# Tail stores from two hardware queues at once, and tail pairs one place earlier

## The chip, the cores and the metric

The kernel runs on one core of a Trainium2 chip. The metric is device time in microseconds (us), the median of several runs. Before the change it is 433.02 us (three runs, 432.55 to 433.25). The profile's span counts from the first to the last instruction and is about 2 us shorter than the device time. Times inside a trace are us from that span's start.

## The reference

Linear attention (8 batches, 8 heads, 576 positions, head size 64) gives `x`. A spectral mixing step with 64 complex modes and 128 weight matrices of 512x512, read from HBM as f32, gives `y`. Then comes a small channel product:

```python
X = np.fft.rfft(x, axis=1)
Yr = einsum(Xr, w_r) - einsum(Xi, w_i);  Yi = einsum(Xr, w_i) + einsum(Xi, w_r)   # 64 modes
u = x + np.fft.irfft(Y, n=576, axis=1)
out = u + np.maximum(u @ w_ch, 0.0)        # [8, 576, 512] f32, 9.4 MB
```

## The kernel before

Each batch has 576 rows. 512 of them make four full tiles (`x_main`, 128 partitions). The 64 left over are the tail: the tails of two batches share one tile (`x_tail`), one batch on partitions 0 to 63, the other on 64 to 127. In the last stage tiles go in pairs: TensorE adds the inverse transform and the channel product in PSUM (`channels`, `rectified`, `finish`), ScalarE applies the relu, VectorE adds to `x`, and a store follows. 16 pairs are main pairs, 2 are tail pairs.

```python
    pairs = []
    for b in range(B):
        pairs += [(b * NJJ, b * NJJ + 1), (b * NJJ + 2, b * NJJ + 3)]
        if b % 4 == 3:
            k = b // 4
            pairs.insert(len(pairs) - 1, (B * NJJ + 2 * k, B * NJJ + 2 * k + 1))
    # ...
    def store(t: int, n_t: int):
        if t < B * NJJ:                       # main: 128 partitions, 4 KB runs for a pair
            b, jj = divmod(t, NJJ)
            nc.sync.dma_start(
                out=out[b, 0:512, :].rearrange("(r j) d -> r j d", j=NJJ)[:, jj : jj + n_t, :],
                in_=x_main[b][:, jj : jj + n_t, :],
            )
            return
        i = t - B * NJJ                       # tail: two stores of 64 partitions, 2 KB runs
        for hf in range(2):
            (nc.sync, nc.gpsimd)[hf].dma_start(
                out=out[2 * i + hf : 2 * i + 4 : 2, 512:S, :].rearrange("b r d -> r b d"),
                in_=x_tail[i // 2][hf * 64 : hf * 64 + 64, :, :],
            )

    def finish(n: int):
        # ... inverse transform; the first and the last pair are stored tile by tile ...
        on_bank(n, {0, 1}, nc.vector.tensor_tensor(out=x, in0=acc, in1=x, op=ALU.add))
        store(t0, 2)
    # ...
    for n in range(4, len(pairs)):
        channels(n)
        rectified(n)
        finish(n - 1)
    finish(len(pairs) - 1)
```

Four of the experiments (e5, e7, e9, e10) touch the warm-up matmuls. These do no useful work; they are there to keep TensorE's granted clock up while the last weights arrive (from 388 to 394 us it is 1.00 with all of them and 0.74 in e5, which leaves part of them out):

```python
            if t == 1 and kk >= NM - 4:
                keep_warm(6)
        if NM - 4 <= kk < NM - 1:
            keep_warm(3)          # twice
```

Of the kernel before, what the change touches and what calls it, by code (L numbers as in the profile page):

```python
# [47 lines left out]
def kernel(  # L48
# [10 lines left out]
    nc = tc.nc  # L59

    B, H, S, Dh = q.shape
# [4 lines left out]
    NJJ = 4  # L66
# [61 lines left out]
    pin = tc.keep_in_program_order  # L128
# [279 lines left out]
    for kk in range(n_early):  # L408
# [5 lines left out]
    x_tail = [  # L414
        sW.tile([128, 2, D], F32, tag="x_tail", bufs=B // 4, name=f"x_tail{i}") for i in range(B // 4)
    ]
# [3 lines left out]
    def x_of(t: int):  # L420
        if t < B * NJJ:
            return x_main[t // NJJ][:, t % NJJ, :]
        i = t - B * NJJ
        return x_tail[i // 2][:, i % 2, :]
# [81 lines left out]
    def add_inverse(n: int, i: int, t: int, half: int, what: int = BOTH):  # L506

        acc = accs[n][:, i]
        mm = lambda o, l, r: on_bank(
            n, {i}, nc.tensor.matmul(o, l, r, start=False, stop=True, skip_group_check=True)  # L510
        )
        if t < B * NJJ:
            parts = [(t // NJJ, slice(0, 128), slice(t % NJJ * 128, t % NJJ * 128 + 128))]
        else:
            p = t - B * NJJ
            parts = [(2 * p + h, slice(h * 64, h * 64 + 64), slice(512, 576)) for h in range(2)]
        for b, r, sel in parts:
            if what == BOTH:
                mm(acc[r, :], inv_sb[:, sel], YZ[b][:, half, :])
                continue  # L520
            if what & EARLY:
                mm(acc[r, :], inv_sb[: 2 * NE, sel], YZ[b][: 2 * NE, half, :])
            if what & LATE:
                mm(acc[r, :], inv0_sb[:, sel], last[:, half, :])

    pairs = []
    for b in range(B):
        pairs += [(b * NJJ, b * NJJ + 1), (b * NJJ + 2, b * NJJ + 3)]
        if b % 4 == 3:
            k = b // 4  # L530
            pairs.insert(len(pairs) - 1, (B * NJJ + 2 * k, B * NJJ + 2 * k + 1))
    N_PRE = 2
    acc_pools: list = []
    users: dict[int, list] = {}
# [1 line left out]
    def on_bank(n: int, banks: set, ins):  # L536
        pin(ins)
        for other, theirs in users.setdefault(n, []):
            if not banks & theirs:
                tc.declare_no_dep(ins.ins, other.ins, reason="the other bank of the pair")  # L540
        users[n].append((ins, banks))
    accs: dict[int, object] = {}

    def channels(n: int):
        pool = acc_pools[n % 4 // 2]
        accs[n] = pool.tile([128, 2, D], F32, tag="acc", bufs=2, name=f"acc{n}")
        for i, t in enumerate(pairs[n]):
            for cols, src in e0_parts(t):
                on_bank(
                    n, {i},  # L550
                    nc.tensor.matmul(  # L551
                        accs[n][:, i, cols], id16, src, start=(cols.start == 0), stop=False,
                        skip_group_check=True,
                    ),
                )

    def rectified(n: int):
        for i, t in enumerate(pairs[n]):
            add_inverse(n, i, t, 1, LATE if n < N_PRE else BOTH)
        for i in range(2):  # L560
            a = accs[n][:, i]
            on_bank(n, {i}, nc.scalar.activation(out=a, in_=a, func=AF.Relu))  # L562

    def store(t: int, n_t: int):
        if t < B * NJJ:
# [5 lines that stand above are left out]
            return  # L571
        i = t - B * NJJ
        for hf in range(2):
            (nc.sync, nc.gpsimd)[hf].dma_start(
                out=out[2 * i + hf : 2 * i + 4 : 2, 512:S, :].rearrange("b r d -> r b d"),
                in_=x_tail[i // 2][hf * 64 : hf * 64 + 64, :, :],
            )

    def finish(n: int):
        acc = accs[n]  # L580
        single = n in (0, len(pairs) - 1)
        t0 = pairs[n][0]
        for i, t in enumerate(pairs[n]):
            if n < N_PRE:
                add_inverse(n, i, t, 0, EARLY)
                add_inverse(n, i, t, 0, LATE)
            else:
                add_inverse(n, i, t, 0)
            if single:
                x = x_of(t)  # L590
                on_bank(n, {i}, nc.vector.tensor_tensor(out=x, in0=acc[:, i], in1=x, op=ALU.add))  # L591
                store(t, 1)
        if single:
            return
        x = x_main[t0 // NJJ][:, t0 % NJJ : t0 % NJJ + 2, :] if t0 < B * NJJ else x_tail[(t0 - B * NJJ) // 2]
        on_bank(n, {0, 1}, nc.vector.tensor_tensor(out=x, in0=acc, in1=x, op=ALU.add))  # L596
        store(t0, 2)

    done = 0
    rows_done = 0  # L600
# [52 lines left out]
    rectified(1)  # L653
    channels(2)
    finish(0)
    channels(3)
    finish(1)
    rectified(2)
    rectified(3)
    finish(2)  # L660
    for n in range(4, len(pairs)):
        channels(n)
        rectified(n)
        finish(n - 1)
    finish(len(pairs) - 1)
    acc_pools[1].release()
# [30 lines left out]
```

## Time and profile before

| What | Value | Where it is read |
|---|---|---|
| weights until about 391 us | DMA share 1.08, 211 GB/s | stretches |
| start of the last weight matmuls | 394.05 us | timeline |
| full-rate stores, 405.3 to 409.3 us | 402 GB/s | stretches |
| VectorE's last add ends | 424.21 us | timeline |
| last store lands | 429.65 us | issue and landing events |

From the start of the last weight matmuls to the last landing it is 35.60 us. I use this length, the "store stage", because the start itself varies from run to run by more than the change can bring (393.86 to 394.99 us in these profiles).

These lines are from the view of stretches of the kernel before. The columns are the stretch, its length, each engine's busy time with its number of instructions, TensorE's granted clock, the DMA share and GB/s.

```profile
405.30:409.30 4.00, 4.00 (x25) 1.57 (x22) 3.56 (x3) 3.10 (x6) 0.00 (x0) 1.00 1.00 402
411.90:415.00 3.10, 3.10 (x16) 1.45 (x15) 2.89 (x4) 2.65 (x6) 0.00 (x0) 1.00 0.88 218
```

With main stores the DMA engines move 402 GB/s. Around the first tail pair they move 218 GB/s although they are 88% busy: the packets are slow, the engines are not idle. The next lines are the timeline of SyncE and GpSimd there (start, duration, engine, line, what is stored).

```profile
410.93 0.68 SPq L574 DMA_DIRECT2D out_dram<-x_tail  x1
412.26 0.33 SPq L567 DMA_DIRECT2D out_dram<-x_main  x1
411.20 0.63 POOL L574 DMA_DIRECT2D out_dram<-x_tail  x1 [10.47 <-DVE x_tail L596]
```

The next are DMA issues of single short windows of the kernel before. The last number is us from issue to landing. In order: the main store before the tail pair, the two halves, the main store after them, and the one issued at 416.14 us.

```profile
out_dram<-x_main SPq DMA_DIRECT2D x1, 512.0 KB, 2.6
out_dram<-x_tail SPq DMA_DIRECT2D x1, 256.0 KB, 3.2
out_dram<-x_tail POOLq DMA_DIRECT2D x1, 256.0 KB, 4.8
out_dram<-x_main SPq DMA_DIRECT2D x1, 512.0 KB, 5.0
out_dram<-x_main SPq DMA_DIRECT2D x1, 512.0 KB, 5.9
```

The time to landing is a gauge of backlog. It goes from 2.6 to 5.0 us across the tail pair and never returns, because TensorE makes a pair every 1.30 us and the DMA engines need about as long to store one.

The two halves do not run together. In the packet records of the trace, SyncE's half has its packets from 412.26 us (mean 158 ns for 2 KB) and GpSimd's from 413.55 us, 2.35 us after its issue.

### The profile page before, as it was taken

Reading aid. Unit: us, or ns where it says so; the run is one execution under the profiler, and the core shown is the slowest. Engines: PE = TensorE matmul, PEld = TensorE weight load, DVE = VectorE, ACT = ScalarE, POOL = GpSimd, SP = SyncE. Lnnn points to the kernel's source line nnn. Section 1 sums busy time; section 2 is a strip of 40 time slices with the busy share of each in tenths; the row PEclk is TensorE's granted clock in tenths of the full one; section 3 lists DMA queues with packets and bytes.
Section 4 is the critical chain, followed back from the end, with each engine's and each line's share of the span. In section 5 each row is a group of like instructions: output and inputs, shape, how many; then the busy total and the mean of one; then the engine's idle time right before and its main releaser. Section 6 shows DMA issues by size and latency. Waiting matters only on the chain. (4 is left out here: it accounts for less than half of the span.)

```text
span 430.9 us, 6215 instructions
## 1 busy us (share of the span) xinstructions
PE 297.7 (69%) x2542; PEld 154.3 (36%) x2542; DVE 176.9 (41%) x334; ACT 147.3 (34%) x228; POOL 92.3 (21%) x166
## 2 busy tenths in 40 slices
PE   0357867787018777677776767667787678997992
PEld 0346656564004233222322223222233226833440
DVE  0699998854004242322322222322223212202793
ACT  3587666631003222222223213222222221302781
POOL 4233232112102222211222112222212221200100
PEclk9996676666559766657658577566555866999997
DMA  8999999999999999999999999999999999993797
GB/s 148 207 208 209 209 209 209 211 213 215 222 211 213 216 212 213 213 213 213 213 214 214 213 213 213 214 214 214 214 214 213 213 213 213 214 213 77 292 330 281
DMA packets 35563, 92.38 MB, mean 214 GB/s; under 512 B 3152, under 2 KB 16336, under 8 KB 35536
## 3 DMA queue, kind: packets, MB, share of 16 engines
q0 software_dynamic: 32016, 82.52, 98.4%
q1 hardware_dynamic: 3520, 9.47, 5.9%
q8 instruction: 20, 0.33, 0.3%
q14 instruction: 7, 0.06, 0.0%
HBM read 164.07 MB, written 9.44 MB: 403 GB/s over the span
## 5 line engine op out<-in xcount | busy, mean ns | idle before, releaser
L468 PE MATMUL eps<-wch,xTw 128*128 128x512 f16 x144 | 61.4, 575 | 3.7 <-DVE xTw L465 3.2
L476 ACT CAST E<-eps 128x512 f16<-128x512 f32 (+1 forms) x40 | 21.3, 544 | 118.8 <-PE eps L468 118.8
L348 PE MATMUL P<-wr,xt_c 128*32 128x512 bf16 (+1 forms) x260 | 45.6, 560 | 23.5 <-DMA wr<-in_moe_w_r_dram 21.5
L348 PE MATMUL P<-wi,xt_c 128*32 128x512 bf16 (+1 forms) x260 | 44.7, 538 | 23.0 <-DMA wi<-in_moe_w_i_dram 23.0
L114 POOL DMA_DIRECT2D wi<-in_moe_w_i_dram x64 | 34.1, 532 | 122.1 <-PE P L348 86.3
L114 POOL DMA_DIRECT2D wr<-in_moe_w_r_dram x64 | 34.1, 532 | 119.0 <-PE P L348 96.8
L453 DVE TENSOR_TENSOR x_main<-nw,rd 128x256 f32<-128x256 f32 x64 | 24.1, 419 | 72.4 <-PE nw L146 72.4
L362 DVE CAST ys<-P 128x512 f16<-128x512 f32 (+1 forms) x33 | 22.5, 681 | 61.6 <-PE P L348 61.5
L348 PEld LDWEIGHTS <-xt_c 128*32 128x32 bf16 x520 | 24.8, 164 | 58.8 <-issue 28.3
L364 ACT CAST ys<-P 128x512 f16<-128x512 f32 (+1 forms) x32 | 18.5, 580 | 72.2 <-PE P L348 72.0
L146 PEld LDWEIGHTS <-qT 64*128 64x128 f16 (+1 forms) x640 | 20.6, 124 | 54.2 <-issue 38.7
L366 PE MATMUL yt<-pick_sb,ys 128*128 128x16 f16 x256 | 17.2, 176 | 32.1 <-DMA pick_sb<-row_pick 21.0
L465 DVE COPY xTw<-xTp 128x512 f16<-128x512 f16 x36 | 15.2, 423 | 46.0 <-PE xTp L463 46.0
L366 PEld LDWEIGHTS <-ys 128*128 128x128 f16 x256 | 13.2, 105 | 53.0 <-issue 24.8
L146 PE MATMUL num<-kv,qT 64*128 64x65 f16 (+1 forms) x320 | 12.9, 217 | 22.0 <-ACT kv L242 17.9
L468 PEld LDWEIGHTS <-xTw 128*128 128x128 f16 x144 | 14.6, 123 | 37.7 <-issue 23.6
L182 ACT ACTIVATE qe<-q 128x1152 f16<-128x1152 f16 x16 | 17.7, 1155 | 22.9 <-DMA q<-in_q_dram 22.9
L211 PE MATMUL qTp<-id,qe 128*128 128x128 f16 x144 | 16.7, 312 | 12.7 <-DVE qe L195 12.3
L460 ACT CAST x16w<-x_main 128x512 f16<-128x512 f32 x32 | 19.8, 619 | 13.0 <-DVE x_main L453 12.4
L265 DVE TENSOR_TENSOR x<-num,rd 128x512 f16<-128x512 f32 x32 | 22.1, 691 | 1.1
L463 PE MATMUL xTp<-id,x16w 128*128 128x128 f16 x144 | 19.5, 278 | 4.0 <-ACT x16w L460 4.0
L562 ACT ACTIVATE acc<-acc 128x512 f32<-128x512 f32 x36 | 19.1, 581 | 5.4 <-PE acc L510 3.8
(65 smaller groups left out, 382.8 us busy)
## 6 DMA issues: line engine op xcount, KB each, us to landing
wr<-in_moe_w_r_dram POOLq DMA_DIRECT2D x64, 512.0 KB, 18.2
wi<-in_moe_w_i_dram POOLq DMA_DIRECT2D x64, 512.0 KB, 18.4
out_dram<-x_main SPq DMA_DIRECT2D x14, 512.0 KB, 4.9
q<-in_q_dram POOLq DMA_DIRECT2D x8, 576.0 KB, 13.3
k<-in_k_dram POOLq DMA_DIRECT2D x8, 576.0 KB, 14.1
v<-in_v_dram POOLq DMA_DIRECT2D x8, 576.0 KB, 16.2
out_dram<-x_main SPq DMA_DIRECT2D x4, 256.0 KB, 4.0
wch<-in_moe_w_ch_dram POOLq DMA_DIRECT2D x1, 512.0 KB, 20.4
```

The source lines that it names most:

```text
L114: nc.gpsimd.dma_start(out=w, in_=src[kk].rearrange("(p dc) e -> p dc e", dc=NDC))
L146: mm = nc.tensor.matmul(num[hpo][orow, c0 : c0 + 65], qT[rows, hpp, h2, cols], kv_sb[rows, hpp, h2, :])
L265: nc.vector.tensor_tensor(out=dst.rearrange("p (o c d) -> p o c d", o=2, c=4), in0=nv[:, :, :, 0:64], in1=rden.unsqueeze(3).broadcast_to([ ...
L348: mm = nc.tensor.matmul(P[i][dc * 32 : dc * 32 + 32, :], xt_cols(dc, t, kk), w[:, dc, i * pw : i * pw + pw], start=(t == 1), stop=(t == 0) ...
L362: nc.vector.tensor_copy(out=dst, in_=P[i])
L366: mm = nc.tensor.matmul(yt_ps[:, ec, kk % 8, :], st[:, ec * 128 : ec * 128 + 128], pick_sb)
L453: nc.vector.tensor_tensor(out=x[orow, o * 256 : o * 256 + 256].rearrange("p (c d) -> p c d", c=4), in0=nv[o][:, :, 0:64], in1=rd_all[b][or ...
L460: nc.scalar.copy(out=x16, in_=x)
L463: nc.tensor.transpose(xT_ps[:, c, :], x16[:, c * 128 : c * 128 + 128], id16)
L468: nc.tensor.matmul(e_ps, xT[:, c, :], wch16[:, c, :], start=(c == 0), stop=(c == NDC - 1))
L476: nc.scalar.copy(out=dst, in_=e_ps[:, cols])
L562: on_bank(n, {i}, nc.scalar.activation(out=a, in_=a, func=AF.Relu))
```

## The change

The intent is to send the two halves of a tail pair together, on SyncE's and ScalarE's queues, which the profile lists as "hardware_dynamic" (GpSimd's is "software_dynamic"). ScalarE's store must not hold up its relus, so both wait until two pairs later. Hence the tail pairs move one place forward, or the second store would not fit in the loop.

```diff
-            pairs.insert(len(pairs) - 1, (B * NJJ + 2 * k, B * NJJ + 2 * k + 1))
+            pairs.insert(len(pairs) - 2, (B * NJJ + 2 * k, B * NJJ + 2 * k + 1))
...
-            (nc.sync, nc.gpsimd)[hf].dma_start(
-                out=out[2 * i + hf : 2 * i + 4 : 2, 512:S, :].rearrange("b r d -> r b d"),
-                in_=x_tail[i // 2][hf * 64 : hf * 64 + 64, :, :],
+            pin(
+                (nc.sync, nc.scalar)[hf].dma_start(
+                    out=out[2 * i + hf : 2 * i + 4 : 2, 512:S, :].rearrange("b r d -> r b d"),
+                    in_=x_tail[i // 2][hf * 64 : hf * 64 + 64, :, :],
+                )
             )
...
-        store(t0, 2)
+        if t0 < B * NJJ:
+            store(t0, 2)
...
         rectified(n)
+        if pairs[n - 2][0] >= B * NJJ:
+            store(pairs[n - 2][0], 2)
         finish(n - 1)
```

## The prediction

> **What bounds the kernel now.** Until about 391 us the core waits for weights: the stretch view from 0 to 391 us has DMA share 1.08 at 211 GB/s, and the chain of waits enters the last stage with a weight landing at 394.0 us. The change does not touch this. In the store stage (400 us to the end) two rates are nearly equal. TensorE makes a pair of tiles (512 KB) every 1.30 us (timeline); stores move 402 GB/s (405.3 to 409.3 us), one pair per 1.3 us. DVE's last add ends at 424.2 us; SyncE's last store is issued at 424.85 us and lands near 429.6 us (DMA issues by window). Early x_main stores land 2.6 to 2.7 us after issue, so about 2.5 us of the end is backlog in the DMA engines.
>
> **Where the backlog comes from.** The last x_main store before the first tail pair lands after 2.6 us, the next after 5.0 us: the tail pair costs 2.3 us, and later stores (4.8 to 5.9 us) never win it back. Cause: each tail half reads 64 partitions. SyncE's half, issued at 410.93 us, moves alone from 412.3 us, its 2 KB packets at 158 ns against 84 to 87 ns for full-partition 2 KB packets; GpSimd's half is issued at 411.20 us but its packets come at 413.5 us. From 411.9 to 415.0 us only 218 GB/s move. The Trainium skill ("SBUF — State Buffer", Door 1: The DMA port swizzle) says partitions 0 to 63 reach half of the ports; the packet times agree. A further 1.1 us (landing 4.8 to 5.9 us) coincides with a 929 ns instruction fetch at 419.6 us, which stays. Around the second tail pair about 0.8 us is lost (estimate: 296 against 400 GB/s over 3 us).
>
> **What the change does.** It removes GpSimd's late start: ScalarE's half goes behind the relu two pairs later, an estimated 0.3 to 0.5 us after SyncE's. Halves in flight together should read all ports. The same page (section "Can I just issue two DMAs to hit both halves?") measured only +6% from this; I expect more, since the slow pace here is the port limit. It adds two DMA issues on ScalarE, about 0.65 us each (SyncE's are 0.63 and 0.68 us). ScalarE is busy 1.07 us of each 1.30 us pair and TensorE needs a relu some 0.5 us after its end, so the first delays TensorE by 0 to 0.3 us; the second follows the last relu. The move leaves TensorE's and DVE's work unchanged, but puts 1 MB of full-partition stores behind the last tail pair.
>
> **Sum.** First tail pair: 2.3 us falls to about 1.0 us; second: 0.8 to about 0.5 us; minus 0.1 us for ScalarE's issue. Gain about 1.5 us, all at the end of the critical path; at most 2.7 us (DVE's 424.2 plus 2.7 us).
>
> Predicted 431.5 us, range 430.2 to 432.9. Faster by over 2%: 0.01; within 2%: 0.98; slower by over 2%: 0.01.
>
> **What would show it.** The x_main store after the first tail pair lands in 3.3 to 4.3 us; the slices there move over 280 GB/s; last store lands under 4.2 us after DVE's last add; that add ends within 0.4 us of 424.2; relu gap after ScalarE's first DMA 0.2 to 0.7 us.
>
> **What would make it wrong.** Halves still serialize (gain under 0.5 us); ScalarE's issue blocks for over 1 us and holds relu and TensorE; halves overlap perfectly (gain 2.5 us).

## The result

The changed kernel took 432.4 us (median of 4, 432.11 to 432.9) against 433.0 us before. The ratio is 0.9988, with a 95% interval of 0.9971 to 1.0006. Ratios here are the mean time of one kernel's runs over that of the other's of the same rounds, so not quite the ratio of the medians quoted. A second timing, in a later set, gave 433.26 us against 433.17, ratio 1.0000 (0.9985 to 1.0015). By their ratios the two timings give a gain of 0.5 and of 0.0 us, and neither is separated from zero.

The profile shows the issue that was intended. These are SyncE's and ScalarE's timelines of the changed kernel.

```profile
409.90 0.68 SPq L575 DMA_DIRECT2D out_dram<-x_tail  x1
409.33 1.07 ACT L562 ACTIVATE acc<-acc 128x512 f32<-128x512 f32 x2 [0.45 <-PE acc L510]
409.91 0.73 ACTq L575 DMA_DIRECT2D out_dram<-x_tail  x1
410.69 1.07 ACT L562 ACTIVATE acc<-acc 128x512 f32<-128x512 f32 x2 [0.28 <-PE acc L510]
```

The two halves are issued 10 ns apart. ScalarE's store is issued while its engine is still busy with a relu, and the next relu waits 0.28 us, where 0.22 us is usual between main pairs.

Yet the DMA queues do not run together. These lines are the DMA view of the changed kernel in two windows (queue, kind: packets, MB, share of 16 engines). The first line is from 411.2 to 412.5 us, the other two from 412.5 to 414.6 us. Queue q1 is SyncE's, q10 ScalarE's.

```profile
q1 hardware_dynamic: 124, 0.25, 94.8%
q10 hardware_dynamic: 144, 0.26, 53.1%
q1 hardware_dynamic: 109, 0.37, 45.9%
```

In the first window there is not one packet of ScalarE's half (its 144 packets are 128 of 2 KB and 16 of 4 bytes). It starts at 412.52 us, when SyncE's is all but done (last end 412.77 us). The gauge answers accordingly. These are DMA issues of the changed kernel, in the order of the five lines shown before:

```profile
out_dram<-x_main SPq DMA_DIRECT2D x1, 512.0 KB, 2.6
out_dram<-x_tail SPq DMA_DIRECT2D x1, 256.0 KB, 3.2
out_dram<-x_tail ACTq DMA_DIRECT2D x1, 256.0 KB, 5.0
out_dram<-x_main SPq DMA_DIRECT2D x1, 512.0 KB, 4.9
out_dram<-x_main SPq DMA_DIRECT2D x1, 512.0 KB, 5.9
```

The first tail pair costs 2.3 us as before (2.6 to 4.9 us), and the step to 5.9 us is there too. VectorE's last add ends 30.20 us after the stage's start (30.16 before), so ScalarE's stores delay no compute. The store stage is 35.34 us in this profile and 36.27 us in that of the second timing, against 35.60 before.

### The profile page after: what moved, and what is told of

Same layout as the page of the kernel before. It is cut to its first block, busy times and chain, and to the rows that moved or that the text cites. A ratio compares the mean times of both kernels' runs of the same rounds, so it can differ in the third digit from the quotient of the medians.

```text
span 430.8 us, 6214 instructions
## 1 busy us (share of the span) xinstructions
PE 298.1 (69%) x2542; PEld 154.6 (36%) x2542; DVE 176.8 (41%) x334; ACT 147.3 (34%) x228; POOL 90.5 (21%) x164
```

## The experiments

Theory A, after the result: a half-partition store is slow because of the partitions it reads, and the two halves still go through the 16 DMA engines one after the other, so the slow pace lasts for both. Rival B: the number or the making of the 2 KB packets costs the time, or ScalarE's descriptors come late.

Four questions follow: what makes the packets slow, what each part of the change does, what the later step to 5.9 us is, and whether anything fixes the tail.

### Other partitions, same bytes (e1_stride2)

```diff
-                    in_=x_tail[i // 2][hf * 64 : hf * 64 + 64, :, :],
+                    in_=x_tail[i // 2][hf::2, :, :],
```

> The changed kernel, but each of the two tail stores reads every second partition (0, 2, 4 ... and 1, 3, 5 ...) instead of partitions 0 to 63 and 64 to 127. The rows land in the wrong places, so the result is wrong on purpose; bytes, packets, queues and order are the same. Theory A (a half-partition store is slow because of the partitions it reads, and the two halves go through the DMA engines one after the other, so the slow pace lasts for both): packets of the first tail pair fall from 138 to 159 ns to under 100 ns, the x_main store after the first tail pair lands under 3.6 us after its issue instead of 4.94 us, and the kernel is 1.2 to 2.4 us faster than the changed kernel. Rival B (256 packets of 2 KB, or the making of their descriptors, cost the time, whatever the partitions): packets stay at about 150 ns or the second half still starts 1.2 us after the first, landing stays at 4.6 us or more, time within 0.5 us of the changed kernel.

Measured: 431.72 us against 433.03 before, ratio 0.9972 (0.9958 to 0.9986); wrong rows. The main store after the tail pair, and the stretch, next to the same stretch of the changed kernel (first line):

```profile
411.20:414.30 3.10, 3.10 (x16) 1.37 (x14) 2.89 (x4) 2.70 (x6) 0.00 (x0) 1.00 0.97 248
411.00:414.10 3.10, 3.10 (x16) 1.43 (x15) 2.95 (x3) 2.65 (x6) 0.00 (x0) 1.00 1.02 396
out_dram<-x_main SPq DMA_DIRECT2D x1, 512.0 KB, 3.3
```

396 GB/s instead of 248 with the same packets, bytes and queues. So the partitions are the cost. The packet records of the first tail pair tell more (in the row of e2, described next, the halves are told apart by order of start, so its offset is rough):

```
kernel           SyncE's packets     the other queue's    other starts after   SyncE's first share
                 mean, ns            mean, ns             SyncE's, us          on one engine, us
before           158 (2 KB)          277 (4 KB, GpSimd)   1.28                 (not comparable)
changed          159                 138                  1.28                 8 x 159 ns = 1.27
stride 2          87                  86                  0.68                 8 x  87 ns = 0.70
quarters (below) 154, then 88         87, then 104        0.62                 4 x 154 ns = 0.62
one queue (e2)   158 (first half)    132 (second half)    1.2 to 1.3           8 x 158 ns = 1.27
```

128 packets over 16 engines are 8 for each engine. In all three kernels of the table with two hardware queues, ScalarE's packets begin when SyncE's first share is through. Descriptors made late at a fixed pace cannot explain it: the number of descriptors is the same in the second and third row, and the offset is half. But the last row shows that this order needs no second queue: with both halves on one queue the second begins just as late. Whether the engines take turns between the queues, or serve the halves in the order of their issue, these runs do not tell apart.

The gain was 1.3 us against the kernel before, but "1.2 to 2.4 us faster than the changed kernel" was expected; by the ratios it is 0.7 us against the changed kernel's first timing and 1.2 us against its second. The step near 416 us, from 3.2 to 5.2 us to landing, was still there.

### Both halves on one queue (e2_both_sync)

```diff
-                (nc.sync, nc.scalar)[hf].dma_start(
+                nc.sync.dma_start(
```

> The changed kernel with both tail halves on SyncE's queue, none on ScalarE's. If the second queue brought nothing at the first tail pair (halves one after the other in any case), the second half's packets start about 1.3 us after the first's, the next x_main store lands 4.9 to 5.6 us after its issue (its issue can be late by SyncE's extra 0.65 us), and the time is within 0.4 us of the changed kernel. If the second queue did bring an overlap there, the store lands 1 us later than in the changed kernel and the kernel is over 0.6 us slower.

Measured: 432.96 us against 433.03, ratio 0.9999 (0.9987 to 1.0012). The next main store lands 4.7 us after its issue, a little under the expected 4.9 to 5.6 and no later than with two queues; the second half starts about as late as expected (table above).

```profile
out_dram<-x_main SPq DMA_DIRECT2D x1, 512.0 KB, 4.7
```

Counted from the issue of the first half, that store lands after 6.11 us, and after 6.27 and 6.24 us in the changed kernel's two profiles. Against the changed kernel the medians differ by 0.6 us in one timing and by 0.3 us the other way in the second. So the second queue brings nothing at the first tail pair.

### The two parts of the change (e3_queues_only, e4_move_only)

```diff
 # e3: the changed kernel with the order of pairs of before
-            pairs.insert(len(pairs) - 2, ...
+            pairs.insert(len(pairs) - 1, ...
         finish(n - 1)
+    store(pairs[len(pairs) - 2][0], 2)
     finish(len(pairs) - 1)
 # e4: the kernel before with the order of pairs of the change
-            pairs.insert(len(pairs) - 1, ...
+            pairs.insert(len(pairs) - 2, ...
```

> The changed kernel's queues (SyncE and ScalarE) with the order of pairs of the kernel before; the last tail store is issued after the loop, before the last two tiles. If the queues do nothing at the first tail pair and only the place of the second counts, the time is within 0.3 us of the kernel before. If the queues gave the 0.5 us, the time is that of the changed kernel.

> The kernel before with the tail pairs moved one place forward, still on SyncE's and GpSimd's queues. If the move gives the 0.5 us, the time is that of the changed kernel; if the queues do, it is that of the kernel before. The store after the first tail pair lands about 5.0 us after its issue in either case.

Measured: queues alone 433.05 us, ratio 0.9995 (0.9982 to 1.0007). Move alone 433.74 us, ratio 1.0010 (0.9998 to 1.0023), store stage 36.75 us. Neither part gains by itself, and the move alone leans to slower: with GpSimd still issuing, its second half landed 6.25 us after its issue. Differences of 0.5 us between these four kernels are within what one kernel shows between two timings, so the split stays open.

### Without the instruction fetch at 419 us (e5_no_fetch)

```diff
-            if t == 1 and kk >= NM - 4:
+            if t == 1 and kk >= NM - 2:
                 keep_warm(6)
-        if NM - 4 <= kk < NM - 1:
+        if NM - 2 <= kk < NM - 1:
             keep_warm(3)          # twice
```

> The changed kernel with 48 fewer TensorE instructions ahead of the store stage: the warm-up matmuls of the modes 60 and 61 are left out, those of 62 and 63 stay. In every run so far a 16 KB instruction fetch of about 930 ns came when TensorE was within 28 instructions of its end, and the store in flight landed 1.2 us later than the trend. Theory: with fewer instructions that fetch never comes; the landing times of the stores after the first tail pair stay at about 4.8 us and fall slowly instead of stepping to 5.9 us, and the kernel is 0.7 to 1.3 us faster than the changed kernel. Rival: the step is not the fetch's, and the landing times still step by about 1 us near 416 us; or TensorE's clock falls without the warm-up and the stage starts later, so that nothing is gained.

Measured: 433.1 us against 433.16, ratio 0.9995 (0.9979 to 1.0011). The first line is the DMA view of the changed kernel from 419 to 420 us. The second is this kernel's from 397.9 to 399 us. The third is this kernel's store issued at 416.66 us, where the changed kernel has 5.9.

```profile
q8 instruction: 1, 0.02, 5.8%
q8 instruction: 1, 0.02, 7.8%
out_dram<-x_main SPq DMA_DIRECT2D x1, 512.0 KB, 4.7
```

The fetch did not vanish: it came at 398.8 us, where no store was waiting (small transfers there landed late, after 3.0 to 3.4 us, but VectorE's last add came 30.22 us after the stage's start, 30.20 in the changed kernel). The step did vanish. Still nothing was gained: the store stage is 35.61 us, between the two profiles of the changed kernel. The second tail pair, which took 1.28 us from the landing before it in the changed kernel's first profile and 1.89 us in its second, now took 2.30 us. This fits a delay of the fetch that overlaps with the slow second tail pair, so that removing one leaves the other. That the fetch holds up one DMA engine of the 16 while the others go ahead would explain this, but the records do not name the engine, so it is inferred. In e1 and e6 the step is 1.9 us over two stores, twice the length of the fetch (0.92 to 0.93 us), which this does not explain.

The rival about TensorE's clock came true in part. These are the stretches just before the last weights, of the changed kernel and of this one:

```profile
388.00:394.00 6.00, 5.13 (x34) 2.02 (x32) 1.31 (x2) 0.00 (x0) 0.00 (x0) 1.00 0.70 141
388.00:394.00 6.00, 5.98 (x32) 2.00 (x31) 1.32 (x2) 0.00 (x0) 0.00 (x0) 0.74 0.72 144
```

The granted clock falls from 1.00 to 0.74 and TensorE is busy to the end of the stretch. Its last weight matmuls start at 394.53 us here and at 394.99 us in e10, against 393.86 to 394.33 us in the ten profiles with all the warm-up (394.27 and 394.31 us in e7 and e9). So the device times of these four kernels can hold a later start as well, and what the fetch costs is better read from the store stage.

### Quarter stores (e8_quarters)

```diff
-        for hf in range(2):
-            pin((nc.sync, nc.scalar)[hf].dma_start(
-                    out=out[2 * i + hf : 2 * i + 4 : 2, 512:S, :].rearrange("b r d -> r b d"),
-                    in_=x_tail[i // 2][hf * 64 : hf * 64 + 64, :, :]))
+        for j in range(2):
+            for hf in range(2):
+                pin((nc.sync, nc.scalar)[hf].dma_start(
+                        out=out[2 * i + hf + 2 * j, 512:S, :],
+                        in_=x_tail[i // 2][hf * 64 : hf * 64 + 64, j, :]))
```

> The changed kernel with each tail half cut into two stores, one per batch pair member, issued in turn on SyncE's and ScalarE's queues: four stores of 64 partitions, 128 KB each. Theory A (on each DMA engine the first queue's share of a store is drained before the other queue gets its turn, and all 16 engines do so in step, so at any time only one half of the partitions is read): ScalarE's first packets now start about 0.6 to 0.7 us after SyncE's instead of 1.28, but packets stay near 150 ns, the first tail pair still takes about 3 us, and the next store lands 4.6 us or more after its issue; time within 0.5 us of the changed kernel. Rival B (ScalarE's descriptors come late, and halves that are in flight together do run at full pace): packets fall under 120 ns on average, the next store lands under 4.2 us after its issue, and the kernel is over 0.5 us faster.

Measured: correct, 432.0 us against 433.16, ratio 0.9968 (0.9947 to 0.9989). My theory A failed here: it expected packets near 150 ns throughout and a landing of 4.6 us or more. The first quarter ran at 154 ns, but the next two at 87 and 88 ns and the last at 104 ns, and the next main store landed after 4.0 us. B's numbers were met, though not its "descriptors come late": the offset is again one share (0.62 us).

What these kernels show together is this. Just after the half of the partitions changes, packets are fast, and later in the same half they are slow. In the changed kernel ScalarE's first 64 packets took 109 ns, its last 64 took 168 ns. The change of queue is not needed for it: with both halves on one queue (e2) the second half took 109 and 156 ns. With quarters most pieces end before the slow part. That packets of both halves are in flight for a short while after the change would explain it; this is inferred. It does not explain the very last packets of ScalarE's half: from 413.5 us these took about 230 ns, although few of them were left and the next main store's 4 KB packets beside them mostly took about 160. And whether the quarters need two queues at all is open: all four on SyncE's queue was not tried.

### A correct form of the stride (e6_interleaved, e7_both)

Rows of the two batches are interleaved over the partitions by zero-padded left operands. Core of the edit:

```diff
+    for h in range(2):     # qz and invz are zero elsewhere
+        nc.vector.tensor_copy(out=invz[:, h, h::2], in_=inv_sb[:, 512:576])
+    # per tail tile: qz[:, h, :, h::2] <- tail columns of q of batch 2i+h; both batches accumulate in num
-            mm(acc[r, :], inv_sb[:, 512:576], YZ[2 * p + h][:, half, :])     # 64 rows each
+            mm(acc, invz[:, h, :], YZ[2 * p + h][:, half, :])                # 128 rows each
-                    in_=x_tail[i // 2][hf * 64 : hf * 64 + 64, :, :],
+                    in_=x_tail[i // 2][hf::2, :, :],
```

e7_both also leaves out the warm-up matmuls of e5.

> A correct form of the stride-2 experiment: the rows of the two batches of a tail tile are interleaved over the partitions (row r of batch h on partition 2r+h) by zero-padded left operands in the tail matmuls, and each tail store reads every second partition. Queues and order as in the changed kernel. If the half-partition pace was the cost, the result is correct, the packets take 84 to 90 ns, the next store lands 3.2 to 3.6 us after its issue, and the time is within 0.4 us of the stride-2 experiment (431.7 us), 0.6 to 1.6 us under the kernel before. If the extra work on VectorE and in PSUM before the store stage costs something, the stage starts later than 394.3 us and the gain is smaller.

> Interleaved rows and the 48 fewer TensorE instructions together. If both causes of the backlog are as told, the last stores land 2.7 to 3.5 us after their issue, the last landing is at most 3.4 us after VectorE's last add, and the kernel is 1.8 to 2.6 us faster than the kernel before (430.4 to 431.2 us). If only one cause is real, it is no faster than the better of the two single experiments.

Measured: e6 432.36 us, ratio 0.9980 (0.9965 to 0.9995), packets 87 to 88 ns, landing 3.3 us. That is 0.8 us under the kernel before, as expected, but 0.6 us above stride 2, where at most 0.4 was expected. e7 432.81 us, ratio 0.9989 (0.9971 to 1.0008), so its expectation failed. Both are correct. The tail pair now takes longer on TensorE: VectorE's last add ends 31.01 us after the stage's start, against 30.20. TensorE's timeline shows the cause. The first line is the second tail step of the changed kernel (the two main matmuls and the four tail ones), the second that of e6 (four tail ones only).

```profile
407.39 1.15 PE L510 MATMUL acc<-YZ,inv_sb 128*128 128x512 f16 x6
407.91 1.03 PE L535 MATMUL acc<-YZ,invz 128*128 128x512 f16 x4
```

Six matmuls with 64-row tails fit in 1.15 us, four of 128 rows take 1.03 us. In the changed kernel the two 64-row matmuls of a tail tile, which fill different halves of the rows, start 4 ns apart; in e6 each of the 128-row ones starts 216 ns after the one before. I had assumed that two half matmuls cost as much as two full ones.

### The last set on one chip (e11_after_again, e8_quarters_again, e9_quarters_no_fetch, e10_stride2_no_fetch)

These are the changed kernel and the quarters unedited, the quarters with the edit of e5, and stride 2 with the edit of e5 (rows wrong).

> The changed kernel once more, unedited, as the base of this set on one chip. Expected 0.2 to 1.0 us under the kernel before, as in its first timing (ratio 0.9988); the x_main store after the first tail pair again lands 4.9 to 5.0 us after its issue, and ScalarE's first packets again follow SyncE's by 1.25 to 1.3 us.

> The four quarter stores once more, unedited. If their gain was real, 0.4 to 1.2 us under the changed kernel in the same rounds, and the x_main store after the first tail pair lands 3.9 to 4.1 us after its issue; if it was the luck of three rounds, no difference over 0.3 us.

> Quarter stores and the 48 fewer TensorE instructions together. If the fetch near 419 us still costs time once the tail pairs cost less, the landing times do not step near 416 us, the last landing is 33.6 to 34.3 us after the last weight matmuls start (34.58 with quarters alone), and the kernel is 0.3 to 0.9 us under the quarters. Rival: the fetch delays one DMA engine only, and the slow second tail pair hides that, as in the run without the fetch, which gained nothing; then no gain over 0.2 us here either.

> The stride-2 tail stores (wrong rows on purpose) and the 48 fewer TensorE instructions together, so that both causes are gone at no extra work. If these two make up the backlog, the last landing is 33.4 to 34.2 us after the last weight matmuls start (34.68 with stride 2 alone), and stores just before the second tail pair land 3.1 to 3.4 us after their issue instead of 4.8 to 5.1 us; the kernel is 1.8 to 2.6 us under the kernel before. If something else holds the last stores, the last landing is still over 34.4 us after.

| Kernel | Median, us (before: 433.17) | Ratio to before | Store stage, us |
|---|---|---|---|
| changed, again | 433.26 | 1.0000 (0.9985 to 1.0015) | 36.27 |
| quarters, again | 431.73 | 0.9968 (0.9953 to 0.9982) | 34.61 |
| quarters, no fetch | 431.72 | 0.9971 (0.9954 to 0.9988) | 34.69 |
| stride 2, no fetch | 431.72 | 0.9962 (0.9947 to 0.9978) | 33.98 |

The changed kernel's expected gain of 0.2 to 1.0 us did not come. The quarters' gain repeats: the means of the six runs each are 431.81 and 433.22 us, 1.4 us under the changed kernel in the same rounds (0.4 to 1.2 was expected). It is the best correct kernel, level with e9, at 0.3% under both. The DMA issues of its first tail pair and of the main store after it (second profile):

```profile
out_dram<-x_tail SPq DMA_DIRECT2D x2, 128.0 KB, 2.4
out_dram<-x_tail ACTq DMA_DIRECT2D x2, 128.0 KB, 3.2
out_dram<-x_main SPq DMA_DIRECT2D x1, 512.0 KB, 3.9
```

Leaving out the fetch adds nothing to the quarters, as its rival said: the second tail pair takes 2.8 us from the landing before it instead of 1.9. (VectorE's last add also came 0.2 us later in the stage, 30.74 against 30.55 us.) With stride 2, where no tail pair is slow, the landings stay at 2.9 to 3.3 us until the second tail pair and the stage is 0.7 us shorter than with stride 2 alone (one profile of each, and the changed kernel's two differ by 0.9 us, so the size is not settled). The expected 1.8 us by device time was not reached (about 1.6 by the ratio); this stage was also the latest to start. Here the last store still lands 3.77 us after VectorE's last add:

```profile
out_dram<-x_main SPq DMA_DIRECT2D x1, 256.0 KB, 3.7
```

With both causes gone that is what is left: 1 MB of main stores issued within 1.2 us, from 424.03 to 425.22 us.

## Why the prediction was right or wrong

The range held the first median (432.4 in 430.2 to 432.9), and "within 2%" was right. But the range's slow end lay 0.1 us under the kernel before, so it held almost no change at all: that it held the median was luck, not the mechanism. The second median, 433.26 us, lies above the range. The forecast gain of 1.5 us did not come: the two timings give 0.5 and 0.0 us by their ratios. Of the five signs named, the three of the overlap failed (landing 4.9 us, not 3.3 to 4.3; 248 GB/s, not over 280; last store 5.1 us after VectorE's last add, not under 4.2), and the two on the engines held (last add within 0.4 us, relu gap 0.28 us). What came is what the prediction had listed first as making it wrong: halves that still serialize. Point by point:

- **What bounds the kernel, and the backlog.** Right. The stage starts and computes as before, the tail pair costs 2.3 us in both kernels, and e1 shows that the partitions cause it.
- **"ScalarE's half goes ... an estimated 0.3 to 0.5 us after SyncE's."** Wrong in the harmless direction: 10 ns.
- **"Halves in flight together should read all ports", so that "2.3 us falls to about 1.0 us".** This is the step that failed. The halves are issued together but do not run together: the first starts alone, and the second follows when the first's share of 8 packets is through on the engines, 1.28 us later. The landing went from 2.6 to 4.9 us, so the loss is 2.3 us, not 1.0. The Trainium skill had said so, and the prediction cited it only to overrule it: "SBUF — State Buffer", section "Can I just issue two DMAs to hit both halves?", measured only +6% for two transfers at once over one. Here the halves came one after the other, and e2 did as well with one queue. "DMA: Bandwidth & Descriptors", section "Queues, rings and completion order", says that an engine drains a whole packet of typically 9 to 17 descriptors from one queue before it turns to the next. A half gives each engine 8 data packets in the profile's counting, which is about one such turn, and the offsets of 1.28, 0.68 and 0.62 us fit that; but with one queue (e2), where there are no turns, the offset is 1.2 to 1.3 us too, so the turns are not shown to be the reason.
- **Second tail pair, "0.8 to about 0.5 us".** Not settled. It took 1.49 us from the landing before it in the kernel before, and 1.28 and 1.89 us in two profiles of the changed kernel. Counting it as a loss of its own is doubtful too: e5 and e9, which gained nothing without the fetch, suggest that it overlaps with the delay of the fetch.
- **The fetch "stays".** Right: 929 ns in both kernels. That its 1.1 us could be won was the expectation of e5, and was not met.
- **ScalarE's issue costs 0.1 us.** Right in size: VectorE's end moved by 0.04 us, the relu gap by 0.06.
- **Floor of 2.7 us after VectorE's last add.** Too low: 3.77 us in e10, since the last pairs' stores queue behind each other.

## What to carry to other kernels

Two stores issued at the same time need not be two stores in flight: look at the packets of each queue, not at the issues. When a store is slow although the DMA engines are busy, compare its packet time with that of a full-partition store of the same packet size; if the partitions are the cause, spread the rows over the partitions, or cut the halves smaller and let the pieces of the two halves alternate (done here on two queues; one was not tried). Delays in one store stream can overlap, so price a fix with the other delay still in place and with it gone.

## What the Trainium skill lacked or had wrong

- "SBUF — State Buffer", section "Can I just issue two DMAs to hit both halves?", calls one transfer spanning all 128 partitions the only way to reach all ports. It does not say that 64 partitions spread over that range do as well, though the same page's port numbering implies it: two stores of 64 partitions with a step of two ran at 87 ns per 2 KB packet (159 ns with 64 neighbouring partitions), at 396 against 248 GB/s over a stretch as long.
- The same section, and the rule on disjoint partition halves in "DMA: Bandwidth & Descriptors", section "Rules for kernel authors", advise against two transfers. For whole halves the runs agree (no gain). Neither says that smaller pieces of the two halves in turn help: quarter stores brought the packets after the first piece to 87 to 110 ns (two profiles) and the kernel to 0.9968 of the time before, twice.
- "DMA: Bandwidth & Descriptors", section "Latency and other measured facts", gives about 0.6 us to the first byte for SyncE's queue and about 1 us for GpSimd's. It does not say from when. A tail half's first packet came 1.33 us after the start of its issue on SyncE (1.17 us for a quarter), but 0.65 us after the end of the issuing instruction in both cases, so the figure agrees if it is counted from there. On GpSimd it came 2.35 us after the start, behind SyncE's half, which tests nothing.
- "Runtime: NRT & Kernel Launch", section "Instruction fetch mechanics", has the fetch of 16 KiB blocks on a DMA queue of the sequencer's own and calls its cost mostly hidden. It does not speak of other transfers. Here the profile lists 20 such packets of the kind "instruction", 0.89 to 0.98 us each in the kernel before, and the store in flight at the last of them took 1.0 us longer to land than the one before it (0.9 to 1.3 us in the other profiles with contiguous halves and this fetch).
